# Uneven zero-fill rows on the GpSimd DMA queue in a decode-attention gradient kernel on Trainium2

## Chip, cores and metric

The kernel runs on one core of one Trainium2 chip. The metric is device microseconds (us) of one execution. Executions of one kernel agree within about 0.3% here, and all timed runs quoted below are fast runs; the six runs that were only looked at once have no state ("unknown") and are used for their traces, not for their times.

## The reference, cut to what matters

The reference computes a layer and its gradients. What counts here is the size of two of its ten outputs.

```
B, Hkv, Sk, Dh = 2, 8, 32768, 128
W = min(4096, Sk // 4)                        # = 4096
k = k_cache[:, :, Sk - W:, :]                 # attention sees only the last 4096 rows
v = v_cache[:, :, Sk - W:, :]
... softmax attention, output projection, a gated feed-forward, x + s * g
... and the vjp of all that
```

The gradients of `k_cache` and `v_cache` (`out_2`, `out_3`) have the full shape of the caches, 134 MB each in bf16. Only the last 4096 of 32768 rows of each of the 16 (batch, head) blocks differ from zero. The kernel therefore writes 2 x 16 regions of zeros, 7.3 MB each, 235 MB of the 327 MB that it moves in all.

## The kernel before

A tile `Z` of zeros, 128 partitions x 7168 bf16 elements, is the source of every zero-fill transfer. One transfer writes 128 rows of 14336 bytes; a region takes four, all regions 128.

```
zlist = []
for o in (out_2, out_3):
    for b in range(B):
        for hk in range(Hkv):
            zreg = o[b, hk, 0:ZR, :].rearrange("(n p f) d -> p n (f d)", n=nz, p=P)   # nz = 4
            for n0 in range(0, nz, ZCH):                                             # ZCH = 1
                zlist.append(zreg[:, n0:n0 + ZCH, :])

def emit_z(n):            # the next n zero-fill transfers, on the SP queue
    ...
    dma(dst[:, 0, :], Z[:])          # dma = nc.sync.dma_start, kept in program order
```

The main loop has 16 groups, one per (head, batch). At each group the SP queue is given, in this order, the loads of the next group's K and V, the stores of the last group's dK and dV, and seven zero-fill transfers.

```
def slot_emission(g_):
    if g_ + LAG < G:
        emit_loads(g_ + LAG)     # K, V on SP; weights of a new head on GpSimd
    if g_ == 1:
        emit_z(ZX)               # eight more
    flush_pending()              # stores of dK, dV (SP) and of the weight gradients (GpSimd)
    emit_z(nzg)                  # seven
```

The weights of the heads, small inputs and weight gradients go through the GpSimd queue (the two feed-forward weights are loaded on SP). Both queues share the core's 16 DMA engines: below, the packets of both together fill 99% of the time of 16 engines.

## Time and profile before

| | before |
|---|---|
| time, median | 789.72 us (4 runs, 788.73 to 790.02) |
| span of the profiled run | 788.1 us |
| data moved | 326.73 MB |
| busy: PE, DVE, ACT, GpSimd | 53%, 39%, 33%, 5% |

The first fence has lines of the page of the kernel before: section 1 (busy time, share, instructions), section 2 (40 slices of the span, tenths of DMA busy, then GB/s), section 3 (DMA queues: packets, MB, share of 16 engines' time) and section 4 (the chain of work that ended last).

```profile
span 788.1 us, 9282 instructions
PE 413.9 (53%) x3646; PEld 265.2 (34%) x3646; DVE 304.0 (39%) x890; ACT 263.3 (33%) x519; POOL 36.7 (5%) x66
...
DMA  8999999999999999999999999999999999999994
GB/s 331 423 430 428 429 420 427 398 429 422 428 419 429 411 429 410 424 426 422 430 406 430 422 426 403 431 422 430 412 422 427 428 422 410 428 427 426 424 427 193
DMA packets 33452, 326.73 MB, mean 415 GB/s; under 512 B 3960, under 2 KB 3968, under 8 KB 8576
...
q1 hardware_dynamic: 27936, 305.67, 92.4%
q0 software_dynamic: 5472, 20.47, 6.5%
q8 instruction: 28, 0.46, 0.2%
...
DMA 81%; PE 6%; DVE 4%; ACT 2%; issue 2%; SPq 0%; POOLq 0%; POOL 0%; DVEq 0%; ACTq 0%
```

No compute engine is near its limit. The DMA line is at nine tenths or more in all slices but the first and the last, and the queues' packets fill 92.4 + 6.5 + 0.2 = 99.1% of the time of 16 engines. The kernel is bound by data movement from end to end; only in the last slice do the engines stop being full (193 GB/s).

The waits of the SP queue say the same: almost all of its waiting is for earlier transfers, very little for a compute engine.

```profile
engine line waited for: us in total, times, longest us
SPq L52 <- DMA out_dram<-Z: 501.2, 120, 6.2
...
SPq L52 <- DVE dV_sb L516: 8.2, 2, 4.1
```

The page does not show how each of the 16 engines ends. The trace does. A full transfer on the SP queue leaves 16 completion times, one per engine (194 transfers of this queue left 3104 packets of 4 bytes, 16 each), so their spread shows how far the engines have drifted apart. These are not a view of the profile; they are the completion records themselves, sorted, for the last zero-fill transfer of the kernel before (us from the start of the span):

```
before, last zero-fill:
773.64 773.89 775.27 775.68 775.79 775.93 776.07 776.49
778.57 779.03 779.25 779.73 779.74 779.97 780.48 786.83
```

Fifteen engines have finished by 780.48 us. One ends at 786.83 us, 6.35 us after the 15th (the last but one to finish), and the kernel ends 1.3 us later. The mean of the 16 is 777.9 us. Every microsecond that the last one needs beyond that is time in which other engines have nothing to do.

This is how it grew (last minus 15th, in us, of the zero-fill transfers nearest to these times): 0.6 at 98, 2.0 at 212, 3.8 at 399, 4.2 at 655, 6.35 at the end. It did not only grow: between 713 and 752 us it stood at 7.4 to 10.6 us and fell back to 6.4 by 756 us.

The packet records show how it happens. Between 248 and 264 us there is only zero-fill. Of 480 packets of 14336 bytes that start there, 451 take 535 to 537 ns (14336 bytes in 0.535 us, 26.8 GB/s). The other 29 are these (start ns, duration ns):

```
248321 553; 248871 568; 249435 544; 249975 569; 250541 568; 251106 559; 251661 549; 252207 564;
252773 576; 253337 549; 253882 539; 254951 549; 255497 540; 256033 559; 256588 540; 257131 547;
257674 555; 258226 540; 258762 549; 259299 549; 259845 559; 260400 559; 260955 549; 261507 548;
262052 540; 262588 559; 263144 549; 263690 573; 263794 744
```

Each entry but the last, which belongs to another engine, starts where the one before ended, within 12 ns, or an ordinary packet later: 248321 + 553 = 248874, and the next starts at 248871. So this is one engine, and nearly every packet on it takes some 15 ns longer than 535. A full zero-fill has 128 packets, eight for each of the 16 completions, so that is 0.12 us each, and the lag in the completion records grows by about as much there (2.95, 3.05, 3.17 and 3.28 us at 253, 258, 262 and 266 us).

### The profile page before, as it was taken

Reading aid. Unit: us, or ns where it says so; the run is one execution under the profiler, and the core shown is the slowest. Engines: PE = TensorE matmul, PEld = TensorE weight load, DVE = VectorE, ACT = ScalarE, POOL = GpSimd, SP = SyncE. Lnnn points to the kernel's source line nnn. Section 1 sums busy time; section 2 is a strip of 40 time slices with the busy share of each in tenths; the row PEclk is TensorE's granted clock in tenths of the full one; section 3 lists DMA queues with packets and bytes.
Section 4 is the critical chain, followed back from the end, with each engine's and each line's share of the span. In section 5 each row is a group of like instructions: output and inputs, shape, how many; then the busy total and the mean of one; then the engine's idle time right before and its main releaser. Section 6 shows DMA issues by size and latency. Waiting matters only on the chain.

```text
span 788.1 us, 9282 instructions
## 1 busy us (share of the span) xinstructions
PE 413.9 (53%) x3646; PEld 265.2 (34%) x3646; DVE 304.0 (39%) x890; ACT 263.3 (33%) x519; POOL 36.7 (5%) x66
## 2 busy tenths in 40 slices
PE   1966853465625664475535753584547753583300
PEld 1833521334322442344323531353233533332000
DVE  4566370353506261453415270634234451551300
ACT  0653450234314341244313440443223531345000
POOL 5000100001000100000000100010000000011000
PEclk9967865668566665676665665666566666565555
DMA  8999999999999999999999999999999999999994
GB/s 331 423 430 428 429 420 427 398 429 422 428 419 429 411 429 410 424 426 422 430 406 430 422 426 403 431 422 430 412 422 427 428 422 410 428 427 426 424 427 193
DMA packets 33452, 326.73 MB, mean 415 GB/s; under 512 B 3960, under 2 KB 3968, under 8 KB 8576
## 3 DMA queue, kind: packets, MB, share of 16 engines
q1 hardware_dynamic: 27936, 305.67, 92.4%
q0 software_dynamic: 5472, 20.47, 6.5%
q8 instruction: 28, 0.46, 0.2%
q14 instruction: 16, 0.13, 0.0%
HBM read 45.62 MB, written 280.50 MB: 414 GB/s over the span
## 4 chain that ended last, share of the span: by engine, by line
DMA 81%; PE 6%; DVE 4%; ACT 2%; issue 2%; SPq 0%; POOLq 0%; POOL 0%; DVEq 0%; ACTq 0%
DMA out_dram<-Z 48%; DMA KV_sb<-in_A_v_cache_dram 13%; DMA out_dram<-dK_sb 11%; DMA KV_sb<-in_A_k_cache_dram 6%; DMA out_dram<-dw_sb 2%; DVE VT_sb L420 1%; PE bk L415 1%; ACT dh_sb L675 1%; PE bk L504 1%; PE sm L534 1%; PE bk L649 1%; DVE mq L438 1%; DVE junk L468 1%; ACT dV_sb L513 0%; PE bk L682 0%
## 5 line engine op out<-in xcount | busy, mean ns | idle before, releaser
L415 PE MATMUL bk<-ident_bf,KV_sb 128*128 128x128 bf16 x1024 | 88.3, 267 | 127.7 <-DMA KV_sb<-in_A_k_cache_dram 126.3
L415 PEld LDWEIGHTS <-KV_sb 128*128 128x128 bf16 x1024 | 83.3, 124 | 130.8 <-DMA KV_sb<-in_A_k_cache_dram 127.5
L418 ACT COPY KT_sb<-bk 128x1024 bf16<-128x1024 bf16 x64 | 60.4, 1031 | 182.8 <-PE bk L415 182.8
L420 DVE COPY VT_sb<-bk 128x1024 bf16<-128x1024 bf16 x64 | 40.4, 684 | 183.7 <-PE bk L415 183.6
L534 PE MATMUL sm<-KV_sb,EUT 128*8 128x256 bf16 x512 | 91.0, 362 | 16.5 <-ACT EUT L525 16.5
L504 PE MATMUL bk<-R,EU 8*128 8x256 bf16 x512 | 64.3, 398 | 47.6 <-DVE EU L487 27.5
L534 PEld LDWEIGHTS <-EUT 128*8 128x8 bf16 x512 | 56.7, 113 | 50.4 <-ACT EUT L525 20.5
L513 ACT CAST dV_sb<-bk 128x256 bf16<-128x256 f32 x128 | 47.1, 382 | 35.0 <-PE bk L504 33.1
L514 DVE CAST dK_sb<-bk 128x256 bf16<-128x256 f32 x128 | 50.7, 417 | 3.5 <-ACT dV_sb L513 3.4
L516 DVE CAST dV_sb<-bk 128x256 bf16<-128x256 f32 x128 | 50.5, 415 | 2.1 <-DMA out_dram<-dV_sb 1.0
L538 DVE TENSOR_SCALAR OdQ_sb<-sm,s 8x256 bf16<-8x256 f32 x16 | 7.5, 472 | 113.1 <-PE sm L534 113.1
L517 ACT CAST dK_sb<-bk 128x256 bf16<-128x256 f32 x128 | 47.7, 389 | 0.6 <-DVE dV_sb L516 0.6
L504 PEld LDWEIGHTS <-EU 8*128 8x128 bf16 x512 | 18.2, 104 | 87.4 <-issue 50.2
L454 ACT ACTIVATE E_q<-bk,nms_rep 128x512 bf16<-128x512 f32 x32 | 21.7, 683 | 70.1 <-DVE nms_rep L447 67.4
L574 ACT COPY Odq_sb<-bk 2x1024 bf16<-2x1024 bf16 x8 | 8.0, 1002 | 71.7 <-PE bk L572 71.7
L473 PE MATMUL sm<-v,C_e 128*128 128x1 f32 x32 | 9.4, 362 | 41.4 <-DVE v L471 41.4
L468 DVE SCALAR_TENSOR_TENSOR junk<-bk,E_q 128x512 bf16<-128x512 f32 x32 | 22.1, 691 | 16.4 <-ACT E_q L454 14.6
L61 POOL DMA_DIRECT2D wo_h<-in_A_wo_dram x8 | 6.1, 766 | 444.6 <-PE bk L554 444.6
L473 PEld LDWEIGHTS sm<-v,C_e 128*128 128x128 f32 x32 | 8.0, 311 | 52.9 <-DVE v L471 52.9
L494 ACT ACTIVATE R<-sm,sv 128x128 bf16<-128x128 bf16 x16 | 5.9, 368 | 52.5 <-DVE R L493 52.5
L487 DVE SCALAR_TENSOR_TENSOR EU<-bk,sv,E_q 128x512 bf16<-128x512 f32 x32 | 22.4, 741 | 0.0
L438 DVE TENSOR_REDUCE mq<-bk 128x1 f32<-128x512 f32 x32 | 20.5, 680 | 0.4 <-PE bk L430 0.4
(201 smaller groups left out, 538.3 us busy)
## 6 DMA issues: line engine op xcount, KB each, us to landing
out_dram<-Z SPq DMA_DIRECT2D x128, 1792.0 KB, 32.1
KV_sb<-in_A_k_cache_dram SPq DMA_DIRECT2D x16, 1024.0 KB, 33.3
KV_sb<-in_A_v_cache_dram SPq DMA_DIRECT2D x16, 1024.0 KB, 31.3
out_dram<-dK_sb SPq DMA_DIRECT2D x16, 1024.0 KB, 32.2
out_dram<-dV_sb SPq DMA_DIRECT2D x16, 1024.0 KB, 30.2
wq_h<-in_A_wq_dram POOLq DMA_DIRECT2D x8, 512.0 KB, 15.3
wo_h<-in_A_wo_dram POOLq DMA_DIRECT2D x8, 512.0 KB, 10.6
out_dram<-dwo_sb POOLq DMA_DIRECT2D x8, 512.0 KB, 10.6
```

What stands on the lines that cost most here:

```text
L415: nc.tensor.transpose(out=t[:, i * P:(i + 1) * P], in_=KV_sb[:, kvi, j0 + i, :], identity=ident_bf[:, :])
L418: nc.scalar.copy(out=dst[:, j0:j0 + n, :].rearrange("p j k -> p (j k)"), in_=t[:, 0:n * P])
L420: nc.vector.tensor_copy(out=dst[:, j0:j0 + n, :].rearrange("p j k -> p (j k)"), in_=t[:, 0:n * P])
L438: nc.vector.tensor_reduce(out=mq[0:QP, sci:sci + 1], in_=S_ts[sci][0:QP, :], axis=AX.X, op=ALU.max)
L468: nc.vector.scalar_tensor_tensor(out=junk[0:QP, :], in0=dP_ts[sci][0:QP, :], scalar=1.0, in1=E_qs[sci][0:QP, :], op0=ALU.mult, op1=ALU.mul ...
L487: nc.vector.scalar_tensor_tensor(out=EU[0:QP, :], in0=dP_ts[sci][0:QP, :], scalar=sv[0:QP, 2:3], in1=E_qs[sci][0:QP, :], op0=ALU.subtract, ...
L504: nc.tensor.matmul(out=banks[r][:, j2 * 2 * Dh:(j2 + 1) * 2 * Dh], lhsT=EUs[sci][32 * r:32 * r + 2 * rep, jj * P:(jj + 1) * P], rhs=R8[32 ...
L513: nc.scalar.copy(out=dV_sb[:, j0:j0 + 2, :], in_=bv[:, :, 0, :])
L514: nc.vector.tensor_copy(out=dK_sb[:, j0:j0 + 2, :], in_=bv[:, :, 1, :])
L516: nc.vector.tensor_copy(out=dV_sb[:, j0:j0 + 2, :], in_=bv[:, :, 0, :])
L517: nc.scalar.copy(out=dK_sb[:, j0:j0 + 2, :], in_=bv[:, :, 1, :])
L534: nc.tensor.matmul(out=OdQ_ps, lhsT=EUT[:, sci * 4 + jj, 32 * r:32 * r + 2 * rep], rhs=KV_sb[:, :, j, :], start=first, stop=last)
```

## The change

Its intent, as far as the code tells: take rows of the first zero region away from the DMA engine that falls behind and give them to the others. It does this with four transfers on the GpSimd queue whose sources have 5, 3, 8 and 4 partitions. Most of the diff is options that stay off by default (`nk15`, `k15w`, `k15s`, `pair`, `wsplit`); those parts are cut.

```diff
 for o in (out_2, out_3):
     for b in range(B):
         for hk in range(Hkv):
+            reg = o[b, hk, 0:ZR, :].rearrange("(r f) d -> r (f d)", r=rows_per_reg)   # 512 rows
+            if ri == 0:
+                AZ = 16
+                zskip = [(reg[0:10, :].rearrange("(a p) f -> p a f", p=5), Z[0:17:4, :].unsqueeze(1).to_broadcast([5, 2, ZF]))]
+                r0 = 10
+                for p0, k in [(20, 3), (64, 8), (0, 4)]:
+                    zskip.append((reg[r0:r0 + k * AZ, :].rearrange("(a p) f -> p a f", p=k),
+                                  Z[p0:p0 + 4 * k - 3:4, :].unsqueeze(1).to_broadcast([k, AZ, ZF])))
+                    r0 += k * AZ
+                while r0 < rows_per_reg:                 # the other 262 rows: 128, 128, 6, on SP
+                    ...
+                    zlist.append((reg[r0:r0 + n_, :], Z[0:n_, :]))
+                ...
... in slot_emission:
+    if g_ == 4:
+        for d_, s_ in zskip:
+            pdma(d_, s_)                                 # GpSimd queue, in program order
... small transfers:
-    nc.gpsimd.dma_start(out=x_bf[:], in_=A_x.rearrange("b s d -> (b s) d"))
+    dma(out=x_bf[:], in_=A_x.rearrange("b s d -> (b s) d"))          # SP; the same for go_bf, out_0, out_1
-    b2T = pro.tile([P, DC], bf16, name="b2T")
-    nc.gpsimd.dma_start(out=b2T[:], in_=B_b2.rearrange("(c p) -> p c", p=P))
+    b2row = pro.tile([1, D], bf16, name="b2row")
+    pdma(out=b2row[:], in_=B_b2.unsqueeze(0))            # one row, turned by four transposes later
... weight loads of a head are held back until the group before has begun (wdep)
```

More of the change, by code (lines that the diff above doesn't have):

```diff
@@ L14 @@
 PSUM = bass.MemoryType.PSUM
-CFG = dict(zch=1, kvbufs=3, nbank=6, hold=8, lag=1, zx=8)
+CFG = dict(zch=1, kvbufs=3, nbank=6, hold=8, lag=1, zx=8, k15w=0)
 @with_exitstack
@@ L56 @@
     WQ = CFG.get("wq", "gpsimd")
+    WSPLIT = CFG.get("wsplit", False)
     def wdma(out, in_):
@@ L60, in wdma @@
             return dma(out, in_)
+        if WQ == "gpsimd":
+            return pdma(out, in_)
         return getattr(nc, WQ).dma_start(out=out, in_=in_)
@@ L105 @@
         ZCH -= 1
+    NK15 = CFG.get("nk15", 0)
+    rows_per_reg = nz * P
     zlist = []
+    k15list = []
+    tiny_dst = []
+    ri = 0
     for o in (out_2, out_3):
@@ L110 @@
             for hk in range(Hkv):
-                zreg = o[b, hk, 0:ZR, :].rearrange("(n p f) d -> p n (f d)", n=nz, p=P)
-                for n0 in range(0, nz, ZCH):
-                    zlist.append(zreg[:, n0:n0 + ZCH, :])
+                reg = o[b, hk, 0:ZR, :].rearrange("(r f) d -> r (f d)", r=rows_per_reg)
[8 more added lines that the diff above has]
+                    while r0 < rows_per_reg:
+                        n_ = min(P, rows_per_reg - r0)
+                        if 16 < n_ < P:
+                            n_ -= n_ % 16
+                        zlist.append((reg[r0:r0 + n_, :], Z[0:n_, :]))
+                        r0 += n_
+                    ri += 1
+                    continue
+                if ri < NK15 and ZCH == 1 and rows_per_reg >= 120 + 8:
+                    k15list.append((reg[0:120, :], Z[0:120, :]))
+                    tiny_dst.append(out_3[B - 1, Hkv - 1, ZR - 1 - len(tiny_dst), 0:17].unsqueeze(0))
+                    r0 = 120
+                    while rows_per_reg - r0 >= P:
+                        zlist.append((reg[r0:r0 + P, :], Z[:, :]))
+                        r0 += P
+                    if r0 < rows_per_reg:
+                        zlist.append((reg[r0:rows_per_reg, :], Z[0:rows_per_reg - r0, :]))
+                else:
+                    zreg = reg.rearrange("(n p) f -> p n f", p=P)
+                    for n0 in range(0, nz, ZCH):
+                        if ZCH == 1:
+                            zlist.append((zreg[:, n0, :], Z[:, :]))
+                        else:
+                            zlist.append((zreg[:, n0:n0 + ZCH, :], Z[:].unsqueeze(1).to_broadcast([P, ZCH, ZF])))
+                ri += 1
     zpos = [0]
+    z_hist = []
     def emit_z(n):
@@ L119, in emit_z, with pdma, emit_k15 @@
                 return
-            dst = zlist[zpos[0]]
+            dst, src = zlist[zpos[0]]
             zpos[0] += 1
-            if ZCH == 1:
-                dma(dst[:, 0, :], Z[:])
-            else:
-                dma(dst, Z[:].unsqueeze(1).to_broadcast([P, ZCH, ZF]))
+            zi_ = dma(dst, src)
+            z_hist.append(zi_.ins.name)
+    PTOKEN = "plq"
+    def pdma(out, in_):
+        i = nc.gpsimd.dma_start(out=out, in_=in_)
+        tc.stamp_issue_order_token(i.ins, PTOKEN)
+        return i
+    k15pos = [0]
+    def emit_k15(n=1):
+        for _ in range(n):
+            if k15pos[0] >= len(k15list):
+                return
+            i_ = k15pos[0]
+            k15pos[0] += 1
+            dst, src = k15list[i_]
+            t_ = pdma(tiny_dst[i_], Z[0:1, 0:17])
+            k_ = pdma(dst, src)
+            if z_hist:
+                for ins_ in (t_, k_):
+                    tc.add_manual_dep(ins_.ins, z_hist[-1],
+                                      mybir.DependencyInfo(mybir.DependencyClass.Sync, mybir.DependencyReason.SCHED_ONLY),
+                                      reason="pace k15 zero-fill")
     ident_bf = const.tile([P, P], bf16, name="ident_bf")
@@ L172 @@
     x_bf = const.tile([B, D], bf16, name="x_bf")
-    nc.gpsimd.dma_start(out=x_bf[:], in_=A_x.rearrange("b s d -> (b s) d"))
+    dma(out=x_bf[:], in_=A_x.rearrange("b s d -> (b s) d"))
     go_bf = const.tile([B, D], bf16, name="go_bf")
-    nc.gpsimd.dma_start(out=go_bf[:], in_=grad_out.rearrange("b s d -> (b s) d"))
+    dma(out=go_bf[:], in_=grad_out.rearrange("b s d -> (b s) d"))
     x_f = pro.tile([B, D], f32, name="x_f")
@@ L212 @@
     b1T = pro.tile([P, FR], bf16, name="b1T")
-    b2T = pro.tile([P, DC], bf16, name="b2T")
-    nc.gpsimd.dma_start(out=b1T[:], in_=B_b1.rearrange("(p r) -> p r", r=FR))
-    nc.gpsimd.dma_start(out=b2T[:], in_=B_b2.rearrange("(c p) -> p c", p=P))
+    b2row = pro.tile([1, D], bf16, name="b2row")
+    pdma(out=b1T[:], in_=B_b1.rearrange("(p r) -> p r", r=FR))
+    pdma(out=b2row[:], in_=B_b2.unsqueeze(0))
     dma(out=w1_sb[:], in_=B_w1.rearrange("(p cc) f -> p cc f", cc=DC))
@@ L255 @@
     fT = pro.tile([P, DC, B], f32, name="fT")
+    tb = ps_tp()
+    for c in range(DC):
+        nc.tensor.transpose(out=tb[:, 2 * c:2 * c + 1], in_=b2row[0:1, c * P:(c + 1) * P], identity=ident_bf[0:1, 0:1])
+    b2T = pro.tile([P, DC], f32, name="b2T")
+    nc.vector.tensor_copy(out=b2T[:], in_=tb[:, 0:2 * DC].rearrange("p (c two) -> p c two", two=2)[:, :, 0])
     nc.vector.tensor_tensor(out=fT[:], in0=fT_ps, in1=b2T[:].unsqueeze(2).to_broadcast([P, DC, B]), op=ALU.add)
@@ L314 @@
     ZX = min(CFG.get("zx", 8), len(zlist) - HOLD)
-    nzg = (len(zlist) - HOLD - ZX) // G
+    nzg = (len(zlist) + 3 - HOLD - ZX) // G
     kv_tiles = {}
@@ L318, with _wdep, tiny_dma, k15_pair @@
     pending = []
+    PAIR = CFG.get("pair", False)
+    K15EVERY = max(1, (G - 2) // max(1, NK15))
+    loaded = set()
+    first_tr_name = {}
+    WDEP = CFG.get("wdep", True)
+    WDEP_BACK = CFG.get("wdep_back", 2)
+    def _wdep(i, hk_):
+        if not WDEP or hk_ == 0:
+            return
+        if WDEP == "z" and len(z_hist) >= WDEP_BACK:
+            tgt = z_hist[-WDEP_BACK]
+        else:
+            g_prev = (hk_ - 1) * B
+            if g_prev not in first_tr_name:
+                return
+            tgt = first_tr_name[g_prev]
+        tc.add_manual_dep(i.ins, tgt,
+                          mybir.DependencyInfo(mybir.DependencyClass.Sync, mybir.DependencyReason.SCHED_ONLY),
+                          reason="delay weight prefetch")
+    K15W = CFG.get("k15w", 0)
+    K15S = CFG.get("k15s", 0)
+    tiny_n = [0]
+    def tiny_dma():
+        i_ = tiny_n[0]
+        tiny_n[0] += 1
+        return pdma(out_3[B - 1, Hkv - 1, ZR - 1 - i_, 0:17].unsqueeze(0), Z[0:1, 0:17])
+    def k15_pair(pairs, dep=None):
+        insts = []
+        for (o_, i_) in pairs:
+            insts.append(tiny_dma())
+            insts.append(pdma(o_[0:120], i_[0:120]))
+        for (o_, i_) in pairs:
+            insts.append(pdma(o_[120:P], i_[120:P]))
+        if dep is not None:
+            for ins_ in insts:
+                dep(ins_)
     def emit_wloads(hk_):
         wq_t = hkp.tile([P, DC, HD], bf16, name="wq_h")
-        wdma(out=wq_t[:], in_=A_wq[:, hk_ * HD:(hk_ + 1) * HD].rearrange("(c p) f -> p c f", p=P))
+        wq_src = A_wq[:, hk_ * HD:(hk_ + 1) * HD].rearrange("(c p) f -> p c f", p=P)
         wo_t = hkp.tile([P, rep, D], bf16, name="wo_h")
-        wdma(out=wo_t[:], in_=A_wo[hk_ * HD:(hk_ + 1) * HD, :].rearrange("(h p) n -> p h n", p=P))
+        wo_src = A_wo[hk_ * HD:(hk_ + 1) * HD, :].rearrange("(h p) n -> p h n", p=P)
+        if hk_ < K15W:
+            k15_pair([(wq_t, wq_src), (wo_t, wo_src)], dep=lambda i__: _wdep(i__, hk_))
+        else:
+            _wdep(wdma(out=wq_t[:], in_=wq_src), hk_)
+            _wdep(wdma(out=wo_t[:], in_=wo_src), hk_)
         w_tiles[hk_] = (wq_t, wo_t)
@@ L342 @@
         emit_loads(g_)
+        loaded.add(g_)
     def hkv_iter(hk):
         def slot_emission(g_):
+            if PAIR:
+                if g_ % 2 == 0:
+                    for gg in (g_ + 1, g_ + 2):
+                        if gg < G and gg not in kv_tiles and gg not in loaded:
+                            emit_loads(gg)
+                            loaded.add(gg)
+                    if g_ == 2:
+                        emit_z(ZX)
+                    flush_pending()
+                    emit_z(2 * nzg)
+                return
             if g_ + LAG < G:
                 emit_loads(g_ + LAG)
+            if g_ == 4:
+                for d_, s_ in zskip:
+                    pdma(d_, s_)
+            if NK15 and g_ >= 1 and (g_ - 1) % K15EVERY == 0:
+                emit_k15(1)
             if g_ == 1:
@@ L414, in hkv_iter @@
                     for i in range(n):
-                        nc.tensor.transpose(out=t[:, i * P:(i + 1) * P], in_=KV_sb[:, kvi, j0 + i, :],
-                                            identity=ident_bf[:, :])
+                        ti = nc.tensor.transpose(out=t[:, i * P:(i + 1) * P], in_=KV_sb[:, kvi, j0 + i, :],
+                                                 identity=ident_bf[:, :])
+                        if gi not in first_tr_name:
+                            first_tr_name[gi] = ti.ins.name
                     if kvi == 0:
@@ L583, in _st5 @@
         def _st5(hk=hk, dwo_sb=dwo_sb):
-            wdma(out=out_5[hk * HD:(hk + 1) * HD, :].rearrange("(h p) n -> p h n", p=P), in_=dwo_sb[:])
-        pending.append(_st5)
+            return (out_5[hk * HD:(hk + 1) * HD, :].rearrange("(h p) n -> p h n", p=P), dwo_sb)
         dwq_sb = hko.tile([P, DC, HD], bf16, name="dwq_sb")
@@ L594, in hkv_iter, with _st4 @@
                 nc.vector.tensor_copy(out=dwq_sb[:, c, :], in_=bo[:, 0:HD])
-        def _st4(hk=hk, dwq_sb=dwq_sb):
-            wdma(out=out_4[:, hk * HD:(hk + 1) * HD].rearrange("(c p) f -> p c f", p=P), in_=dwq_sb[:])
+        def _st4(hk=hk, dwq_sb=dwq_sb, st5=_st5):
+            o5, t5 = st5()
+            o4 = out_4[:, hk * HD:(hk + 1) * HD].rearrange("(c p) f -> p c f", p=P)
+            if hk < K15S:
+                k15_pair([(o5, t5), (o4, dwq_sb)])
+            else:
+                wdma(out=o5, in_=t5[:])
+                wdma(out=o4, in_=dwq_sb[:])
         pending.append(_st4)
@@ L608 @@
     flush_pending()
+    emit_k15(len(k15list))
     emit_z(len(zlist))
@@ L624 @@
     nc.vector.tensor_tensor(out=o_bf[:], in0=o_f[:], in1=x_bf[:], op=ALU.add)
-    wdma(out=out_0.rearrange("b s d -> (b s) d"), in_=o_bf[:])
+    dma(out=out_0.rearrange("b s d -> (b s) d"), in_=o_bf[:])
     df = tl.tile([B, D], f32, name="df")
@@ L653 @@
                 nc.vector.tensor_copy(out=dw2_sb[:, i, :], in_=bo[:, 0:D])
-        wdma(out=o8[:, r0:r0 + n, :], in_=dw2_sb[:, 0:n, :])
+        (dma if WSPLIT else wdma)(out=o8[:, r0:r0 + n, :], in_=dw2_sb[:, 0:n, :])
     t = ps_st()
@@ L687 @@
                 nc.vector.tensor_copy(out=dw1_sb[:, fq * FQW:(fq + 1) * FQW], in_=bo[:, 0:FQW])
-        wdma(out=o6[:, cc, :], in_=dw1_sb[:])
+        (dma if WSPLIT else wdma)(out=o6[:, cc, :], in_=dw1_sb[:])
     sc = ps_sch()
@@ L708 @@
     nc.vector.tensor_tensor(out=dx_bf[:], in0=u[:], in1=go_bf[:], op=ALU.add)
-    wdma(out=out_1.rearrange("b s d -> (b s) d"), in_=dx_bf[:])
+    dma(out=out_1.rearrange("b s d -> (b s) d"), in_=dx_bf[:])
 _INS = ['A_x', 'A_k_cache', 'A_v_cache', 'A_wq', 'A_wo', 'B_x', 'B_w1', 'B_b1', 'B_w2', 'B_b2', 'grad_out']
```

## The prediction

> **What bounds the kernel now.** The DMA engines. The page gives a span of 788.1 us with 326.73 MB moved; the packets (section 3) fill 99.1% of 16 engines' span, while PE is busy 53%, DVE 39%, ACT 33%. The chain of waits is 81% DMA, 48% the zero-fill (out_dram<-Z); the SP queue waits 501 us for Z and some 10 us for compute. So only DMA work counts, and of it that of the engine that ends last.
>
> Each transfer leaves 16 completion times in the trace, one per engine. For the last zero-fill they run from 773.64 (first) over 777.5 (median) and 780.48 (15th) to 786.83 us (last). One engine falls behind throughout: 2.8 us behind the first at 92 us, 8.2 at 395, 13.2 at the end. In steady stretches it needs about 4.37 us for a zero-fill, the others 4.26. It alone sets the last 6.3 us. Instruction fetches are a suspect, not a shown cause.
>
> **What the change does.** With its options at their defaults the k15 and pair branches are dead. Left are: (a) 250 of the 512 rows of the first zero region go by four GpSimd transfers of 5, 3, 8 and 4 source partitions; (b) the four 2-row transfers move from GpSimd to SP; (c) b2 is loaded as one row and turned by four transposes; (d) weight loads and stores keep program order and weights are held back.[...] (a) gives engines 0-3 18 rows each, engine 4 two, the others 16[...]. With the other 262 rows (16 per engine, 6 single rows on engines 0-5), engine 4 gets 13 rows fewer than before's 32, engines 0-3 three more, 5 one more.
>
> **Cost.** A 14336-byte row takes 0.535 us. Engine 4: -13 x 0.535 = -7.0 us; engines 0-3: +1.6 us. If the laggard is engine 4, it ends near 779.9, and the end moves to the 15th, 780.5, or to 782.1 if that is among engines 0-3. Two extra SP issues ahead of the first weight load, 0.43 us each: +0.9 us. b2's 2-byte elements made 16 packets of about 0.95 us, one per engine: -0.9 us. Transposes: off the path. (d) costs nothing: about 30 us of transfers are queued ahead. Sum: 786.8 becomes about 781.5, gain 5.3 us.
>
> **Prediction: 784.3 us**, range 780.5 to 790.8. Faster by over 2%: 0.02; within 2%: 0.96; slower by over 2%: 0.02. About one in four: the spared engine isn't the laggard, and the time is 789.5 to 791.5.
>
> **What the profile would show.** Right: the spread of the last zero-fill's 16 completions falls from 13.2 to 7-9 us, the step from 15th to last (6.3 us) gone; during the GpSimd zero-fill (between 90 and 200 us) one engine gains some 7 us on the others; MB unchanged; the SP queue still waiting for Z. Wrong: an outlier 6 us or more behind remains, or a new one.
>
> **What would make it wrong.**[...] the laggard differs between runs; the few-partition transfers run slower than 0.535 us a row; the two output rows at the end of the SP queue add a completion latency[...]; held-back weights starve PE and then SP.

Cut from it, and marked, are a rule for how transfers on the GpSimd queue are spread over the engines, which no run had shown, with the reason for (b) and a risk that rested on it, and a figure for a latency. The rows per engine are assumption, not a reading of a trace. Engine 4 was to go from 786.8 to 779.9 us by 13 rows fewer, which leaves the end to the next one, at 780.5 us, or at 782.1 with three rows more; with +0.9 and -0.9 us for the other parts that came to about 781.5 us, a gain of 5.3.

## The result

| | before | after |
|---|---|---|
| time, median | 789.54 us (13 runs, 788.73 to 790.15) | 784.79 us (9 runs, 783.79 to 785.65) |
| span of the profiled run | 788.1 us | 782.7 us |
| data moved | 326.73 MB | 326.73 MB |
| last completion of a big transfer | 786.83 us | 781.47 us |
| mean of that transfer's 16 completions | 777.9 us | 778.2 us |

The ratio is 0.994, with a 95% interval of 0.993 to 0.9949. Ratios here are the mean time of one kernel's fast runs over that of the other's fast runs of the same rounds, so not quite the ratio of the medians in the table. The change is faster by 0.6%, which is well outside the noise.

Lines of the page after, from the same sections as before:

```profile
span 782.7 us, 9288 instructions
PE 409.8 (52%) x3650; PEld 261.1 (33%) x3650; DVE 303.2 (39%) x891; ACT 263.6 (34%) x519; POOL 37.5 (5%) x66
...
DMA  8999999999999999999999999999999999999997
GB/s 346 408 426 426 423 421 427 400 428 424 424 405 430 426 423 428 406 429 427 423 401 429 424 427 423 414 426 423 431 406 431 424 430 411 432 427 423 421 430 315
DMA packets 33928, 326.73 MB, mean 417 GB/s; under 512 B 4436, under 2 KB 4444, under 8 KB 9052
...
q1 hardware_dynamic: 27676, 302.10, 92.1%
q0 software_dynamic: 6208, 24.05, 7.6%
q8 instruction: 28, 0.46, 0.2%
...
DMA 78%; PE 10%; DVE 4%; ACT 3%; issue 1%; SPq 0%; ACTq 0%; DVEq 0%
```

The bytes are the same, 3.6 MB of them moved from q1 (SP) to q0 (GpSimd), and the slices are as full as before. Only the last slice differs: 315 GB/s instead of 193. The view by stretches of time shows it more sharply. First the end of the kernel before, then the end of the changed one; the last two numbers of a line are the mean DMA share and GB/s.

```profile
760.00:774.00 14.00, 0.00 (x0) 0.00 (x0) 0.00 (x0) 0.00 (x0) 0.00 (x0) 0.50 1.00 422
774.00:788.10 14.10, 0.00 (x0) 0.00 (x0) 0.00 (x0) 0.00 (x0) 0.00 (x0) 0.50 0.25 105
```

```profile
755.00:769.00 14.00, 0.00 (x0) 0.00 (x0) 0.00 (x0) 0.00 (x0) 0.00 (x0) 0.50 1.00 426
769.00:782.70 13.70, 0.00 (x0) 0.00 (x0) 0.00 (x0) 0.00 (x0) 0.00 (x0) 0.50 0.64 268
```

In the last 14 us of the kernel before, the 16 engines are busy for a quarter of the time, in the last 13.7 us of the changed one for two thirds. The SP queue still waits for the same things (one line of each kind):

```profile
SPq L52 <- DMA out_dram<-Z: 500.8, 120, 7.1
...
SPq L52 <- DVE dK_sb L647: 4.3, 1, 4.3
```

And the completion records of the last big transfer (here the store of dV comes last in the queue):

```
after, last store of dV:
775.06 775.22 775.84 776.11 776.21 776.82 778.28 778.46
778.64 778.81 779.33 779.65 780.17 780.21 780.80 781.47
```

The engine that stood alone is gone; the last one is 0.67 us behind the 15th. The mean did not move (777.9 and 778.2 us), because the work is the same. The gain is the last engine coming nearer to the mean.

The moment of it can be seen too. The four uneven transfers were issued at 91.3 to 93.1 us and had landed by 147.3 us. In a zero-fill issued at 79 us, before them, the first two engines end within 0.06 us of each other; in one issued at 131 us, the first is 4.87 us ahead of the second and 6.35 us ahead of the eighth; the prediction had some 7 us. One engine has been let off.

The completion records of the uneven transfers show how they fell. Each has 16 completions. In the one of 3 partitions thirteen come at 120.32 to 123.06 us and three at 129.82 to 130.07; in the one of 8, five at 129.26 to 131.09 and eleven at 136.81 to 139.26; in the one of 4, one at 138.10 and fifteen at 144.11 to 147.28. So 3, then 3 + 8, then 3 + 8 + 4 engines are late: the three transfers of 16 rows per partition fell on 15 different engines and left one out.

### The profile page after: what moved, and what is told of

Read it like the earlier page. It is cut to its first block, busy times and chain, and to the rows that moved or that the text cites. A ratio compares the mean times of both kernels' runs of the same rounds, so it can differ in the third digit from the quotient of the medians.

```text
span 782.7 us, 9288 instructions
## 1 busy us (share of the span) xinstructions
PE 409.8 (52%) x3650; PEld 261.1 (33%) x3650; DVE 303.2 (39%) x891; ACT 263.6 (34%) x519; POOL 37.5 (5%) x66
## 2 busy tenths in 40 slices
DMA packets 33928, 326.73 MB, mean 417 GB/s; under 512 B 4436, under 2 KB 4444, under 8 KB 9052
## 4 chain that ended last, share of the span: by engine, by line
DMA 78%; PE 10%; DVE 4%; ACT 3%; issue 1%; SPq 0%; ACTq 0%; DVEq 0%
DMA out_dram<-Z 45%; DMA KV_sb<-in_A_k_cache_dram 11%; DMA KV_sb<-in_A_v_cache_dram 8%; DMA out_dram<-dV_sb 8%; DMA out_dram<-dK_sb 4%; PE sm L667 2%; DMA out_dram<-dw_sb 1%; PE bk L546 1%; ACT dh_sb L814 1%; DVE VT_sb L553 1%; PE bk L637 1%; PE bk L788 1%; PE bk L831 1%; DVE junk L601 1%; ACT dV_sb L646 1%
## 5 line engine op out<-in xcount | busy, mean ns | idle before, releaser
L546 PE MATMUL bk<-ident_bf,KV_sb 128*128 128x128 bf16 x1024 | 84.4, 258 | 139.9 <-DMA KV_sb<-in_A_k_cache_dram 138.6
L546 PEld LDWEIGHTS <-KV_sb 128*128 128x128 bf16 x1024 | 78.9, 120 | 143.1 <-DMA KV_sb<-in_A_k_cache_dram 140.0
L667 PE MATMUL sm<-KV_sb,EUT 128*8 128x256 bf16 x512 | 89.2, 358 | 15.4 <-ACT EUT L658 15.4
L168 POOL DMA_DIRECT2D out_dram<-dwo_sb x8 | 6.1, 765 | 623.6 <-ACT dwq_sb L724 566.9
## 6 DMA issues: line engine op xcount, KB each, us to landing
KV_sb<-in_A_v_cache_dram SPq DMA_DIRECT2D x16, 1024.0 KB, 31.4
```

The lines of the kernel that those rows point to most:

```text
L546: ti = nc.tensor.transpose(out=t[:, i * P:(i + 1) * P], in_=KV_sb[:, kvi, j0 + i, :], identity=ident_bf[:, :])
L667: nc.tensor.matmul(out=OdQ_ps, lhsT=EUT[:, sci * 4 + jj, 32 * r:32 * r + 2 * rep], rhs=KV_sb[:, :, j, :], start=first, stop=last)
```

## The experiments

Theory L: one DMA engine, number 4, falls behind (it is called the straggler below), and the uneven rows relieve it. Rival R: the gain comes from the rest of the change. In two of the expectations "the cursor" is the name for an assumption: that the few-partition transfers on GpSimd take the engines in turn, each as many as it has partitions. The completions above (3 + 8 + 4 different engines) agree with it, and four_first tests it. Rows per engine, in the expectations and in the comments of the diffs, are the plan under this assumption, starting at engine 0; no trace gives the rows of a numbered engine. How the engines are numbered is told at probe_before. Further questions are how the engines are chosen, why one falls behind, and whether a better distribution gains more. "Before" is timed anew in each series.

### The change without the uneven rows

```diff
-                if ri == 0:
+                if False:           # and zskip = []
```

> The changed kernel with everything of the change kept except the uneven zero-fill: the first zero region is written like all others, 32 rows per DMA engine. Theory L (one DMA engine lags, the uneven rows relieve it): the gain is gone, the time is 789 to 790.5 us and the last zero-fill transfer again ends with one engine some 6 us behind the 15th. Rival R (the gain comes from the rest: b2 in one row, small transfers on the SP queue, later weight loads): the time stays at 784 to 786 us.

Measured: 789.47 us (789.28 to 789.85, 5 runs) against 789.68 us of before; ratio 1.0, interval 0.9988 to 1.0013. Lines of its page, span and the slices of section 2:

```profile
span 787.5 us, 9285 instructions
...
GB/s 352 409 424 430 425 421 424 405 429 426 425 409 429 423 427 399 429 426 424 428 406 428 424 426 398 431 425 426 416 416 427 427 427 408 428 425 427 425 429 216
```

The weak last slice is back (216 GB/s), and in the last zero-fill the 15th engine ends at 781.53 and the last at 786.32 us. Everything else in the change is worth nothing together, within the interval of about 1 us either way. Rival R falls.

### Only the uneven rows, on the kernel before

```diff
 (kernel before)
+ the uneven first region, its four transfers on GpSimd at g_ == 4, as in the change
-    nc.gpsimd.dma_start(out=x_bf[:], ...)        # the same for go_bf
+    dma(out=x_bf[:], ...)
```

> The kernel before plus only the uneven zero-fill and the two input-row loads on the SP queue[...]; b2, weight loads and output rows as before. Theory L: 784 to 786 us. Rival R: 789 us or more.

Measured: 784.09 us (783.64 to 784.32, 5 runs); ratio 0.9931, interval 0.9918 to 0.9943. The last store ends at 781.34 us, the 15th engine at 780.64. The uneven rows bring the whole gain. The trace shows that their four transfers did not go out together as in the change: in the same order, but at 11.6, 31.4, 92.2 and 92.8 us, with weight loads between them. The gain does not hang on the time of their issue.

### The same, with the 2-row loads left on GpSimd

```diff
 (only_spare)
-    dma(out=x_bf[:], ...)                         # the same for go_bf
+    nc.gpsimd.dma_start(out=x_bf[:], ...)
```

> As only_spare, but the two 2-row input loads stay on GpSimd ahead of the uneven transfers. If a 2-row transfer moves the cursor by 2, the spared engine is number 8 instead of 4, and engine 4 gets 35 rows instead of 32: theory L expects 790 to 792 us, slower than before, with the lagging engine 7 us or more behind the 15th at the end. If the cursor theory is wrong, or it does not matter which engine is spared, 784 to 786 us as in only_spare.

Measured: 783.47 us (782.97 to 785.39, 5 runs); ratio 0.9931, interval 0.9918 to 0.9945. The last store ends at 779.87, the 15th engine at 779.11 us. The expectation was a miss: with the two 2-row loads ahead of them in the GpSimd queue, the uneven transfers still relieve the straggler, so these loads did not shift them to other engines. Why not is not shown. Each of the two loads reports 16 completions (in the trace of before), but so does every transfer on the GpSimd queue, the uneven ones of 5, 3, 8 and 4 partitions too; on this queue the count does not tell which engines carried the data. So the reason for part (b) of the change, keeping the 2-row loads from shifting the uneven transfers to other engines, was wrong, and that part was not needed.

### Another engine spared

```diff
 (changed kernel)
-  5 partitions x 2 rows, then 3 x 16, 8 x 16, 4 x 16      # engine 4 gets 2 rows
+  8 partitions x 2 rows, then 8 x 16, 7 x 16              # meant: engine 7 gets 2 rows
```

> The changed kernel with three uneven transfers of 8, 8 and 7 source partitions[...]; total and queue the same. Theory L with engine 4 as the laggard: engine 4 has two rows more than before, 789.5 to 791.5 us. If merely moving rows to the GpSimd queue, or sparing any engine, brings the gain: 784 to 786 us. If engine 7 were the laggard: 783 to 785 us, and the changed kernel's own gain would need another reason.

Measured: 790.08 us (789.66 to 790.3, 5 runs); ratio 1.0007, interval 0.9995 to 1.002. The last store of dV:

```
spare_7:
773.44 773.92 774.80 775.74 776.75 776.80 776.84 777.50
778.82 779.04 779.05 780.32 781.53 781.54 781.96 787.22
```

The straggler is back at 787.22 us, 5.3 us behind the 15th, although 256 rows go through the GpSimd queue, where the change sends 250, and one engine is meant to be relieved of 14 rows, where the change takes 13 from engine 4. It matters which engine is relieved.

### The same four transfers in another order

```diff
 (changed kernel)
-  (0, 5 partitions, 2 rows), (20, 3, 16), (64, 8, 16), (0, 4, 16)     # first source partition, count, rows
+  (0, 4, 16), (0, 5, 2), (20, 3, 16), (64, 8, 16)
```

> The changed kernel with the same four uneven transfers, from the same source partitions, but the one of 4 partitions first. If a cursor hands out the DMA engines, each transfer taking the next k of them, engines 0 to 3 get 16 rows from the first transfer and 16 more from the last, engines 4 to 8 only 2: engines 0 to 3 then carry 49 rows of the region instead of 32, the end moves to them and the time is 789 to 794 us. If the engine follows from the source partition, nothing changes: 784 to 786 us.

Measured: 794.76 us (794.36 to 795.1, 4 runs) against 788.99 us; ratio 1.007, interval 1.0053 to 1.0087. The last store of dV:

```
four_first:
771.51 773.19 773.53 773.63 774.98 777.41 778.88 780.72
781.63 781.71 782.05 784.36 789.52 790.44 790.74 791.36
```

Exactly four engines end late, as they must if the first and the last of the four transfers both fell on engines 0 to 3. The source partitions were the same as in the change, so the engine does not follow from the partition: the order of the transfers decides. The assumption that the transfers take the engines in turn agrees with this run (four engines late, 794.76 us) and with the completions of the change; spare_moved shows that not every transfer of the queue counts. The time is 0.8 us above the upper end of what was expected.

### Which engine is the straggler

A 2-row transfer on the SP queue left three completion updates in the trace of the change and the 6-row one seven: one 0.40 to 0.46 us after the issue, and later one for each row. So a small piece of k partitions behind a large transfer gives the times of k engines out of the large one's 16. The numbers of the engines are labels: engines 0 to k-1 are those of a piece of k, and engine k is the one that a piece of k + 1 adds. That a longer piece keeps the engines of the shorter one is the author's assumption; the pairs below agree with it. In four_first this places two of the four late engines: the 2-row store behind the last store reports 790.61 and 790.91 us, so engines 0 and 1 are among them. The last row of the zero-fill was cut into such pieces, one after each of the late zero-fill transfers.

```diff
 (kernel before; last row of the zero-fill taken out)
+    probes = [(n * 32 elements of that row, Z[0:n, 0:32]) for n in range(2, 16)]
     dma(dst, src)                      # each of the late zero-fill transfers
+    dma(*probes[...])                  # then a piece of n partitions on the same queue
```

> The kernel before, with the last row of the zero-fill written in small pieces of 2, 3, ... 15 partitions, one after each of the late zero-fill transfers on the same queue.[...] Theory: the engine that is last by 6 us or more is missing from the pieces of 2 to 4 partitions and present in those of 5 and more, so it is engine 4. If it is another engine, the sparing of engine 4 needs another reason. The time itself means little here, up to 5 us more.

Measured: 793.1 us, one look. Two neighbouring pairs from the completion records (a large transfer, then the piece behind it):

```
probe_before:
zero-fill 700.89 701.01 701.72 701.81 702.37 703.68 703.81 703.86 704.45 705.02 708.23 708.86 709.76 709.96 713.26 719.24
4 pieces  701.91 704.21 704.78 710.28
zero-fill 707.73 707.83 708.63 708.67 709.25 710.52 710.59 710.69 710.72 711.01 713.77 714.52 715.24 715.36 718.70 725.80
5 pieces  708.81 710.95 711.38 715.74 726.28
```

The straggler (719.24, then 725.80) is not among engines 0 to 3, and it is the one that the piece of five adds (726.28). The other four entries are those of the piece of four, 5.5 to 6.9 us later, as the entries of the second zero-fill are later than those of the first by 5.4 to 6.9 us. It is engine 4, the engine that the change was built to spare.

> The changed kernel with the same pieces. Theory: engine 4 is no longer last at the end; engines 0 to 3 have been moved back by 3 rows, 1.6 us, against the other engines of their half. No rival for the order; the reading is meant to show which engines set the end now.

Measured: 790.26 us, one look. In the changed kernel with the same pieces, the last engine of the last store ends at 787.01, and the 2-row store behind it reports 784.40 and 787.18: the last one is now engine 0 or 1, which the change has given three more rows each. In the unprobed profile of the change the two rows' completions are 779.82 and 780.38 while the last store ends at 781.47, so there another engine is last. The straggler is gone in both; which engine comes last after it is not the same.

### Why engine 4 falls behind

```diff
 (kernel before)
- all loads, all compute
+ the zero-fill as it is, and zeros in all other outputs        # wrong result on purpose
```

> Wrong result on purpose: no loads and no compute, all outputs written with zeros in about the same transfers (280 MB). If the lagging engine is slow in itself, its packets are stretched here too and it ends 7 us or more behind the 15th. If it is slowed by what the compute engines' instructions bring along (fetches and the like), the stretched packets are gone and the 16 engines end within 2 us. About 665 to 690 us (280 MB at the 26.8 GB/s of a packet on each of 16 engines).

Measured: 671.86 us, result wrong as intended, one look. The zero-fill landing at 654.69 us has its first completion at 654.26: after 650 us of streaming, all 16 engines are within 0.43 us. Engine 4 is not slow in itself. Something that the rest of the kernel brings along slows it.

Two more kernels add the instructions of some engines to this one. Nothing waits for them, and no data moves for them but their own instructions.

```diff
 (zeros_only)
+    3600 matmuls of 128x128 on PE                              # zeros_pe
```

> Wrong result on purpose: zeros_only with 3600 matmuls on PE beside the transfers, which no transfer waits for. If the stream of instructions of PE is what slows one DMA engine, one engine's packets are stretched again and it ends some microseconds behind the others while PE works; else the 16 engines end within 1 us as in zeros_only.

Measured: 683.08 us, 11.2 us more than zeros_only, one look. The page: busy slices of PE, the DMA lines, and the queues.

```profile
span 681.2 us, 7422 instructions
...
PE   8999999999991000000000000000000000000000
...
DMA  8999999999999999999999999999999999999991
GB/s 334 420 419 420 423 420 425 424 421 424 421 423 426 429 431 427 428 426 428 423 423 426 425 426 425 426 425 425 429 425 425 425 424 425 423 423 425 427 419 36
...
q1 hardware_dynamic: 24768, 280.51, 97.9%
q8 instruction: 28, 0.46, 0.2%
```

For comparison, zeros_only:

```profile
span 670.1 us, 221 instructions
...
GB/s 335 426 423 428 420 425 430 421 428 420 430 420 427 428 422 429 422 429 421 426 428 423 427 422 425 424 427 421 429 420 429 421 426 429 422 429 422 427 420 265
...
q1 hardware_dynamic: 24768, 280.51, 99.3%
q14 instruction: 1, 0.01, 0.0%
```

Both kernels send the same 24768 packets through q1. With PE at work in the first third of the span, the last slice falls from 265 to 36 GB/s: one engine is finishing alone. Its lag over the 15th engine, from the completion records:

```
zeros_pe:  landed at us   43.9   77.2  110.6  145.9  179.3  209.7  229.2  400.9  656.9
           last - 15th us  0.7    2.7    5.1    7.3    9.7   11.2   10.9   10.7   10.1
```

The lag grows evenly while PE works, stops when PE stops at about 206 us, and then stays at 10 to 11 us. The packets show it as in the kernel before: between 95 and 101 us nearly every packet on one engine takes 578 to 601 ns, one after the other (95700 601; 96297 578; 96871 587; 97446 587; 98035 595; 98627 578; 99201 596), while the other engines' packets of this size take 561 ns at most in those microseconds, apart from the one behind an instruction fetch (942).

So the work of PE slows one DMA engine. 7200 PE instructions (3600 matmuls and as many weight loads) cost it 11 us, about 1.5 ns each. Whether it is the number of instructions that counts or the time that PE is busy was not tested, and the number of the slowed engine was not probed in this run.

The kernel before agrees with PE as the cause. PE is idle there from 124.9 to 144.8 us, and in the four zero-fill transfers that land in that stretch the straggler is 1.42, 1.41, 1.42 and 1.45 us behind the 15th; at 212 us, with PE at work again, it is 1.99. DVE and ACT are idle there too (two DVE operations), so this stretch alone does not tell the three apart.

Two things happen here, and only one of them is the straggler. The page gives q8 as a queue for instructions; zeros_only has no packet on it, and this run, with 7200 PE instructions, has 28 of 16384 bytes, one every 7 us while PE works. They are taken for PE's instruction fetches here, one for 257 instructions. Each takes 0.9 us of some engine and is followed by a packet stretched by about 0.4 us. In the completion records engines other than the last take these steps of about 0.5 us in turn, until the 15th is 3.3 us behind the first at 179 us. That is what spreads the other 15, not the straggler: from 45 to 210 us the straggler falls a further 0.1 to 0.4 us behind the first engine with every transfer, whether a fetch falls into it or not.

```diff
 (zeros_only)
+    900 operations of 128x512 on DVE, 600 copies on ACT        # zeros_dve_act
```

> Wrong result on purpose: zeros_only with 900 operations on DVE and 600 on ACT beside the transfers. The same question for these two engines: an engine that falls behind while they work would show that their instructions bring the lag; 16 engines within 1 us would clear them.

Measured: 672.25 us, 0.4 us more than zeros_only, one look. In the transfers nearest to 100, 210, 400 and 655 us the last engine is 0.85, 0.42, 0.74 and 0.35 us behind the 15th, where zeros_only has 0.01 to 0.07. This measure hides that two engines are late: at 655 us the last three end at 654.63, 656.05 and 656.40 us, so two are 1.4 and 1.8 us behind the 14th, more than the 1 us that was to clear DVE and ACT. The even growth of zeros_pe is not seen, though. Each step up of the last engines, by 0.4 to 1.1 us, comes within 6 us of one of the 12 instruction packets (q14, 8192 bytes each) that this run has more than zeros_only, and between most steps the lag shrinks. So what DVE and ACT bring here comes with their fetches. A drift at PE's 1.5 ns per instruction would be 1.4 us for 900 DVE operations (an estimate from zeros_pe), too little to tell from the steps, so these engines are neither cleared of a drift nor convicted of one.

What stays open is the mechanism: no run shows what PE's work makes one DMA engine do. Nor does any show whether the recording of the profile has a part in it: every run reports spans and clocks, so none shows the kernel without any recording.

### Another distribution of the rows

The mean of the 16 completions, 778.2 us, is what a perfect distribution would reach, 3.3 us before the last one of the change. From the order in probe_after a plan was made.

```diff
 (changed kernel)
-  (0, 5, 2), (20, 3, 16), (64, 8, 16), (0, 4, 16)        # 35 rows of the region on engines 0-3, 32 on 8-15
+  (0, 5, 2), (20, 3, 14), (64, 8, 19), (0, 4, 13)        # 31 on engines 0-3, 35 on 8-15
```

> The changed kernel with the rows of the first zero region handed out anew, after the completion times of probe_after: engines 0 to 3 get 31 rows of it (35 in the change), engine 4 18 (19), engines 5 to 7 30 (33, 32, 32), engines 8 to 15 35 (32). Theory: what is left of the spread is the half of engines 0 to 7 against 8 to 15, so the last completion moves ahead by 1.5 to 2 us, and the time is 782.5 to 783.5 us, about 1% below before. If the order of the engines at the end changes from run to run, or something else sets the end, 784 to 786 us as the change.

Measured: 785.08 us (784.19 to 785.59, 5 runs); ratio 0.9939, interval 0.9925 to 0.9952. No gain over the change. The last store ends at 782.27 us, the mean is 778.6 us.

> The balanced kernel with the small pieces of probe_before. It was expected to gain 2 us on the change and gained nothing. If the order of the engines is stable and only my sizes were off, engines 8 to 15 (3 rows more, 1.6 us) are now the last ones in the pieces, and engines 0 to 7 the first. If the order changes from kernel to kernel, the engines that were ahead in probe_after and those that are ahead here, less the 1.6 us and 2.1 us moved on purpose, are not the same.

Measured: 789.97 us, one look. In these two pairs of the late transfers

```
probe_balanced:
zero-fill 731.28 733.07 734.00 734.22 734.40 734.51 735.00 736.35 736.92 737.27 738.31 739.16 739.51 739.64 740.79 740.82
9 pieces  734.22 734.76 735.05 735.37 736.91 737.49 737.77 739.70 739.84
zero-fill 736.94 739.15 739.70 739.81 740.15 740.49 740.63 741.23 741.74 741.86 742.85 743.41 743.78 743.98 745.15 745.58
10 pieces 739.89 740.02 740.33 740.80 741.40 741.94 742.07 743.97 744.18 746.13
```

the last one (745.58) is absent from engines 0 to 8 and is added by engine 9. In probe_after engine 9 was in the middle: behind the zero-fill that ended between 737.41 and 747.24, the entry that engine 9 adds to the piece of ten is 742.29 or 743.25, some 4 us or more before the last. Three more rows (3 x 0.535 us) explain 1.6 us of that, not the rest. So both branches of the expectation hold in part: engines of the half that was given more rows now end last, and the order also shifts by microseconds between kernels. Planning for the other 15 engines from one trace is planning for that trace. Why the order shifts was not tested; the fetches, whose steps fell on engines other than the last in turn in zeros_pe (about 0.5 us each), are a candidate.

## Why the prediction was right

- **What bounds the kernel.** Right. The DMA engines, and of them the one that ends last. In no_spare and spare_7 that engine is left alone and the time is before's; where it is relieved, the time falls.
- **The size.** Right. The last completion was to move from 786.8 to about 781.5 us; it moved to 781.47. The time was to be 784.3 us; it is 784.79. That both are so close is in part luck: the medians differ by 4.75 us, not the 5.3 us of the sum, executions of the change spread over 1.9 us, and the engine that ends last in the profiled one was not foreseen (below).
- **Engine 4.** The prediction left one chance in four that the spared engine is not the straggler. probe_before and spare_7 show that it is. That this is the engine which the uneven transfers leave out was assumed too, with no run behind it; the outcome bears it out (the last completion at 781.47 instead of 786.83 us).
- **Which engine ends last now.** Half right. Engines 0 to 3 with three more rows were to set the end if the 15th was one of them. In probe_after engine 0 or 1 did; in the unprobed profile another engine did. The sum of it, an end between 780.5 and 782.1 us, held.
- **The spread.** A little below the prediction: 6.5 us in the last zero-fill, where 7 to 9 us was expected and 13.2 was before; from the 15th to the last, 0.67 instead of 6.35 us.
- **The rest of the change.** Its sum was right, nothing: +0.9 us for two issues ahead of the weight load and -0.9 us for b2 were to cancel, and no_spare is at 789.47 against 789.68 us. The two terms were not measured one by one. In the trace the first weight load is issued at 1.42 us instead of 0.74, which is 0.7 us, not 0.9. The 16 packets of b2 take 0.62 to 1.20 us in the trace of before, 0.94 on average, with up to 12 in flight at once, so they were on at least 12 engines; in that of the change the 16 packets of the row take 0.011 us each.
- **The reason for the SP loads.** Wrong. The author held that the 2-row loads had to leave the GpSimd queue because they would shift the uneven transfers to other engines. spare_moved keeps them there and is as fast (783.47 us).
- **The fear of another spared engine.** The author feared that the engine which the uneven transfers leave out would change from one execution to the next. It did not come true: all executions of the change lie between 783.79 and 785.65 us, where spare_7, made to spare another engine, is at 789.66 to 790.3. Why it does not change was not looked at.
- **The suspect.** The prediction named instruction fetches as a suspect for the straggler. In zeros_pe it is the work of PE that makes one engine fall behind, while the steps that come with the fetch packets are seen on the other engines in turn. That the straggler of the kernel has the same cause rests on zeros_only and on its standing still while PE is idle.

## What to carry to other kernels

When a kernel is bound by DMA and every slice is full, look at the 16 completion times of a late transfer before anything else: the difference between the last and the mean is at most the time that a better distribution can win, here 9 us of 790 (the change won 4.75), and a single engine behind the others could be relieved here by writing one region unevenly. Find out by probes which engine it is, since rows taken from another won nothing here (spare_7, 790.08 us), and check on the trace that the transfers fall on the engines that you think. Stop when the straggler is gone; the remaining order of the engines shifted from kernel to kernel by microseconds, and 3.3 us were left to win.
